# Three stages on one core: loads of the gates, decays as bias, transposes in pieces and the first units in another order

## The chip, the core and the metric

The kernel runs on one core of a Trainium2 chip. The metric is the time of one execution on the device, in microseconds (us). The core has TensorE (PE, its weight loads are PEld), VectorE (DVE), ScalarE (ACT), GpSimd (POOL) and SyncE (SP), which here issues every DMA. Each engine works through its own list of instructions in order and waits for others by semaphores.

## The reference

Three stages in a row, all in fp32. The first is an mLSTM over 4 batches of 8 heads (32 rows), 768 tokens, 40 channels:

```python
for t in range(S):
    m_new = np.maximum(f_gate[:, :, t] + m, i_gate[:, :, t])
    f_stab = np.exp(f_gate[:, :, t] + m - m_new)
    i_stab = np.exp(i_gate[:, :, t] - m_new)
    m = m_new
    C = f_stab * C + i_stab * einsum('bhd,bhe->bhde', v_t, k_t)
    n = f_stab * n + i_stab * k_t
    y[:, :, t] = sigmoid(o_gate_t) * (C q_t) / max(|n . q_t|, 1)
```

The result, as 3072 tokens of 320 channels, goes through a soft mixture of experts (logits with phi, a softmax over the tokens that fills 32 slots, 8 experts of 4 slots with a relu network of width 1024, a softmax over the slots that brings them back) and then through x -> relu(x W_in)^2 W_out with a width of 2048.

## The kernel before

The recurrence is computed in chunks of 128 tokens, 6 of them. In a chunk the state is not stepped: scores k.q of all pairs of tokens are multiplied by a matrix of decays and masked (causal), then multiplied by v; what comes from earlier chunks is added from a state of 40 x 41 per row. The 32 rows are in 11 groups of up to 3; a group and a chunk make a unit, 66 in all. The units of groups 0 and 1 come first, two chunks of one and two of the other in turn (units 0 to 11), then group after group.

Ahead of that stands the preparation `prep` for a pair of chunks (steps are named by a digit for the pair, 1 to 3, and a letter). Gates of all 32 rows lie on partitions three times over (96), tokens along the free axis. "f" (L359) is a scan of forget gates, "i" (L375) the input gates less it, "m" (L365) the running maximum, "h" (L387) its negative cast to bf16, "p" (L370) the maximum before the chunk. "b" and "a" (L375) subtract the chunk's last and previous maximum, "B" and "A" (L378) are the exponentials of that. "r" (L381), "u" (L394), "l" (L375) and "v" (L396) make the parts of the maximum in bf16 that TensorE will broadcast. "q" transposes everything to tokens on partitions (two matmuls L355, copied by ScalarE at L356 into `qt3`): columns 0 to 31 are the biases of the decay exponentials, 32 to 63 the weights of the values, 64 to 95 the decays of the earlier state. D0 to D2 (`prep_dec`, L403 to L423) make the states' decays.

For a unit n: Mn broadcasts the maximum (TensorE, L448, three matmuls), En takes three exponentials with a bias from `qt3` (ScalarE, L462), Kn masks them (GpSimd, L469), Tn are the scores (TensorE, L479), pn their product (VectorE, L491, "P"), Un and Cn the state's update (TensorE L510, VectorE L526 and L541, decays masked on GpSimd L557), W the values times their weights (GpSimd, L435). Products with the values (L582) are done for two units together, those with the state (L567) for each; L603, L612 and L619 add them. L701 is the tanh that makes the sigmoid of the output gates.

The order of all engines in this first part is written by hand: a loop over the units does M of unit i+3, T of i+2, U of i+1, then a slice of the string START, then P of i+2, E of i+3 and the rest. The string's first part, up to the first bar, runs ahead of the loop, each further part in one iteration. "~n" are n warm-ups: matmuls of the identity whose result is never read (L203). From unit 12 on the string plays no part. Later the spare time of the engines is filled with steps of the second and third stage and with weights cast ahead.

Loads go in program order into one queue. Keys are loaded into a block-diagonal form (`kbd`, 120 partitions, three blocks), whose zeros VectorE (L285) and ScalarE (L288) write first.

Of the kernel before, what the change touches and what calls it, by code (L numbers as in the profile page):

```python
# [13 lines left out]
AF = mybir.ActivationFunctionType  # L14
# [3 lines left out]
NEG = -1e30  # L18
# [14 lines left out]
W8 = 1  # L33
WO = (3, 6, 9)
LAST = {3: "PADNgGG", 2: "gGGA", 1: ""}
START = "~36 1f 1i 1m 1h 1p 1b 1aG 1B 1r 1u 1A 1v D0 2f 1l T0 T1 1q M0 2i E0 W0 K0 D0 M1 E1 ~6 2m D0 2p 2b 2aG K1 W2 P0 2h D0 2B 2r 2u U0 P1 M2 2v E2 2A 2l K2 C0 ~7 | 3f 3i D1 ~6 | D1 2q 3m 3h 3p | D1 3b 3aG 3B 3r | 3u D1 3A 3l 3v | D2 3q | D2 | D2 | D2 X |"
REBIAS = 2.0**-112


# [5 lines left out]
def kernel(  # L45
# [240 lines left out]
    for g, cs in ((1, halves[0]), (0, halves[1]), (1, halves[1])):
        z = kbd[g][:, :, cs]
        nc.scalar.activation(z, ident[0 : 3 * D, 0:1].unsqueeze(2).to_broadcast(list(z.shape)), AF.Copy, scale=0.0)  # L288
    for g in range(2):
        load_kb(g, halves[0])  # L290
        load_q(g, halves[0])
        load_kv(g)
    for g in range(2):
        load_kb(g, halves[1])
        load_q(g, halves[1])
    nc.sync.dma_start(out=phs, in_=phi)
    load_x(0, range(NC))
# [4 lines left out]
    )  # L302

    rst = gt(96, [NC, L])
    nc.gpsimd.memset(rst, 1.0)
    nc.gpsimd.memset(rst[:, :, 0:1], 0.0)
    dl = gt(96, [NC, L])
    nc.gpsimd.memset(dl, 0.0)
    nc.gpsimd.memset(dl[:, 0, 0:1], NEG)
    mprev = gt(96, [NC, 1])  # L310
    nc.gpsimd.memset(mprev, NEG)
    nc.gpsimd.memset(hm, 1.0)
    nc.gpsimd.affine_select(
        out=hm, in_=hm, pattern=[[-D, 3]], compare_op=ALU.is_ge, fill=0.0, base=0, channel_multiplier=1
# [6 lines left out]
        nc.gpsimd.memset(rmask[32 * r : 32 * r + 32, r : r + 1], 1.0)  # L321
    nc.gpsimd.memset(selJ, 0.0)
    nc.gpsimd.tensor_copy(selJ[:, :, 0:8], ident[0:32, 0:32].rearrange("p (j i) -> p j i", j=4))
    nc.vector.tensor_reduce(out=gmask, in_=gj, axis=AX.X, op=ALU.add)
    nc.vector.tensor_reduce(out=gs3, in_=gj.rearrange("p g j -> p j g"), axis=AX.X, op=ALU.add)
    nc.vector.tensor_copy(hsel, gs3.unsqueeze(2).to_broadcast([32, 3, D]))
    for r in range(4):
        rs = slice(32 * r, 32 * r + 32)
        nc.vector.tensor_copy(selF[rs, :], ident[rs, rs])
    nc.vector.tensor_copy(sel96, selF[0:96])  # L330

    def flat(t):
        return t.rearrange("p c s -> p (c s)")
# [65 lines left out]

    def prep_dec(c0, c1):  # L400
# [1278 lines left out]
```

## Time and profile before

| | us |
|---|---|
| median of 3 runs | 376.63 (375.51 to 376.94) |
| profiled execution | 376.6 |
| its span (first to last instruction) | 374.9 |
| TensorE busy | 364.6 (97%) |
| VectorE busy | 263.5 (70%) |
| ScalarE busy | 258.5 (69%) |
| GpSimd busy | 102.8 (27%) |
| chain that ended last, TensorE's share | 85% |

Busy times are sums over the whole span; GpSimd works in the first half only. TensorE's share counts the warm-ups as work, and the granted clock is 1.00 throughout. The chain follows the last instruction back, at each step to what released it. The stretch that the change touches is the first 30 us or so; a row of the timeline gives the start, the duration, the line and the operation of one or several instructions of the same form.

### The profile page before, as it was taken

How to read it: one execution, taken by the hardware profiler on the slowest of the kernel's cores; microseconds unless marked ns; L12 is line 12 of the kernel's file. 1: busy time of each engine (PE TensorE's matmuls, PEld its weight loads, DVE VectorE, ACT ScalarE, POOL GpSimd, SP SyncE). 2: the span in 40 equal slices, each digit the busy share in tenths (PEclk: the TensorE clock that was granted, in tenths of full speed). 3: DMA queues.
4: the chain of work that ended last, by engine and by line, in shares of the span. 5: the costliest groups of instructions: out<-in, count | busy, mean ns of one | idle time of the engine just before them, and what ended most of it. 6: DMA issues, size and time to landing. Idle time of an engine off the chain costs nothing.

```text
span 374.9 us, 10814 instructions
## 1 busy us (share of the span) xinstructions
PE 364.6 (97%) x4203; PEld 325.1 (87%) x4203; DVE 263.5 (70%) x597; ACT 258.5 (69%) x594; POOL 102.8 (27%) x205
## 2 busy tenths in 40 slices
PE   8999999998899999999999999999999999999996
PEld 6789888888779885345999999999999999999995
DVE  8879889986998587886799655555555555555551
ACT  7798776678566865766798756676675666667661
POOL 5576986775687573000000000000000000000000
PEclk9999999999999999999999999999999999999999
DMA  5887998999979999893000200020020001002002
GB/s 183 266 315 217 344 328 238 298 332 347 295 199 397 311 353 365 313 380 130 2 0 2 70 3 0 2 71 2 0 72 1 0 11 60 3 0 73 0 2 70
DMA packets 23004, 56.73 MB, mean 151 GB/s; under 512 B 2865, under 2 KB 9865, under 8 KB 22569
## 3 DMA queue, kind: packets, MB, share of 16 engines
q1 hardware_dynamic: 22953, 56.04, 44.3%
q8 instruction: 33, 0.54, 0.6%
q14 instruction: 18, 0.15, 0.1%
HBM read 52.10 MB, written 3.93 MB: 149 GB/s over the span
## 4 chain that ended last, share of the span: by engine, by line
PE 85%; DVE 5%; ACT 4%; POOL 3%; issue 2%; POOLq 0%
PE ps_mb L1574 19%; PE ps_st L1574 17%; PE ps_lt L1574 9%; PE ps_st L479 8%; PE ps_o L1501 4%; PE ps_o L567 4%; PE ps_o L582 4%; PE ps_st L1389 2%; PE ps_m L1501 2%; ACT w L462 2%; POOL w L469 2%; PE ps_mb L448 2%; PE ps_lt L203 2%; PE ps_st L510 2%; PE ps_lt L733 2%
## 5 line engine op out<-in xcount | busy, mean ns | idle before, releaser
L1525 DVE CAST hi<-ring 128x512 fp32r<-128x512 f32 x93 | 39.7, 427 | 62.0 <-ACT ring L1524 51.8
L1526 DVE TENSOR_TENSOR los<-ring,hi 128x512 fp32r<-128x512 f32 x96 | 66.6, 693 | 9.8
L462 ACT ACTIVATE w<-ps_mb,qt 128x128 f32<-128x128 f32 x192 | 56.4, 368 | 11.5 <-PE ps_mb L448 7.0
L1506 ACT ACTIVATE ring<-ps_o 128x512 f32<-128x512 f32 x64 | 38.2, 597 | 35.0 <-PE ps_o L1501 35.0
L1524 ACT ACTIVATE ring<-ring 128x512 f32<-128x512 f32 x93 | 58.8, 632 | 3.0
L479 PE MATMUL ps_st<-par 120*128 120x128 f32 (+1 forms) x384 | 57.0, 284 | 0.7 <-DVE cu L541 0.6
L1574 PE MATMUL ps_mb<-wohlh,hi 128*128 128x320 f32 x160 | 49.4, 310 | 0.0
L1574 PE MATMUL ps_mb<-wohll,hi 128*128 128x320 f32 x160 | 49.3, 309 | 0.0
L1574 PE MATMUL ps_mb<-wohlh,los 128*128 128x320 f32 x160 | 49.2, 309 | 0.0
L479 PEld LDWEIGHTS ps_st<-par 120*128 120x128 f32 (+1 forms) x384 | 47.9, 191 | 1.2 <-PE ps_mb L448 0.9
L491 DVE TENSOR_TENSOR p<-ps_st,w 128x384 f32<-128x384 f32 (+1 forms) x66 | 35.6, 539 | 16.8 <-POOL w L469 8.2
L469 POOL TENSOR_SCALAR_AFFINE_SELECT w<-w 128x384 f32<-128x384 f32 (+1 forms) x66 | 38.3, 581 | 25.1 <-ACT w L462 23.6
L1574 PE MATMUL ps_st<-wohll,hi 128*128 128x320 f32 x144 | 44.6, 310 | 0.0
L1574 PE MATMUL ps_st<-wohlh,hi 128*128 128x320 f32 x144 | 44.5, 309 | 0.0
L1574 PE MATMUL ps_st<-wohlh,los 128*128 128x320 f32 x144 | 44.5, 309 | 0.0
L1506 ACT ACTIVATE ring<-ps_m 128x512 f32<-128x512 f32 x32 | 19.1, 598 | 19.1 <-PE ps_m L1501 19.1
L1574 PEld LDWEIGHTS ps_mb<-wohll,hi 128*128 128x128 f32 x160 | 29.9, 187 | 1.5
L1574 PEld LDWEIGHTS ps_mb<-wohlh,hi 128*128 128x128 f32 x160 | 30.0, 188 | 0.0
L1574 PEld LDWEIGHTS ps_mb<-wohlh,los 128*128 128x128 f32 x160 | 30.0, 188 | 0.0
L1574 PEld LDWEIGHTS ps_st<-wohll,hi 128*128 128x128 f32 x144 | 27.0, 187 | 2.1 <-issue 0.6
L1574 PEld LDWEIGHTS ps_st<-wohlh,los 128*128 128x128 f32 x144 | 27.1, 188 | 0.0
L1574 PEld LDWEIGHTS ps_st<-wohlh,hi 128*128 128x128 f32 x144 | 27.1, 188 | 0.0
(318 smaller groups left out, 762.2 us busy)
## 6 DMA issues: line engine op xcount, KB each, us to landing
ring<-in_w_dram SPq DMA_DIRECT2D x32, 320.0 KB
stage<-in_w_in_dram SPq DMA_DIRECT2D x10, 512.0 KB
par<-in_w_dram SPq DMA_DIRECT2D x6, 640.0 KB
ring<-in_w_dram SPq DMA_DIRECT2D x6, 640.0 KB
out_dram<-ring SPq DMA_DIRECT2D x24, 160.0 KB
par<-in_k_s_dram SPq DMA_DIRECT2D x9, 360.0 KB
x<-in_o_gate_dram SPq DMA_DIRECT2D x9, 320.0 KB
par<-in_k_t_dram SPq DMA_DIRECT2D x23, 120.0 KB
```

Source lines behind the costliest of these rows:

```text
L462: nc.scalar.activation(w[:, j, :], mb[:, 128 * j : 128 * j + 128], AF.Exp, bias=qt3[:, c, h0 + j : h0 + j + 1])
L469: nc.gpsimd.affine_select(out=w, in_=w, pattern=[[0, nh], [1, 128]], compare_op=ALU.is_ge, fill=0.0, base=0, channel_multiplier=-1)
L479: nc.tensor.matmul(st[:, 128 * j : 128 * j + 128], lhsT=kbd[g % 2][0:nd, j, ts_], rhs=qin[g][0:nd, ts_], start=True, stop=True,)
L491: nc.vector.tensor_tensor(out=p, in0=sts.pop((g, c))[:, 0 : nh * 128].rearrange("p (n t) -> p n t", n=nh), in1=ws.pop((g, c)), op=ALU.mult,)
L567: nc.tensor.matmul(pos[g, c // 2][:, o0 : o0 + nv], lhsT=qin[g][0:nd, 128 * c : 128 * c + 128], rhs=cbds[g, c - 1][0:nd], start=True, stop ...
L582: nc.tensor.matmul(po[t0 : t0 + 32, o0 : o0 + DV], lhsT=p[:, j, t0 : t0 + 32], rhs=vin[g][:, c, j, :], start=True, stop=True,)
L1501: nc.tensor.matmul(t, lhsT=gst[n][:, 128 * k : 128 * k + 128], rhs=cst[tg], start=True, stop=True)
L1506: nc.scalar.activation(r, t, AF.Relu)
L1524: nc.scalar.activation(r, r, AF.Square)
L1525: nc.vector.tensor_copy(hi, r)
L1526: eng.tensor_tensor(out=lo, in0=r, in1=hi.bitcast(F32), op=ALU.subtract)
L1574: nc.tensor.matmul(acc[u][:, 0:DM], lhsT=l_[:, 128 * u : 128 * u + 128], rhs=wohl[r_, f // 8][:, f % 8, :], start=(f == 0 and a == 0), sto ...
```

## The change

It has these parts. The gates of the first two chunks are loaded alone and first, those of the other four behind the first keys and queries; keys, queries and values come in parts of two and four chunks. The zeros are written in smaller pieces, a part of them by GpSimd. The differences "a" and "b" go: the exponentials take the maximum as a bias per partition, and for that run chunk by chunk (32 x 128); "n" makes the negative of the last maximum. The transposes "q" become three pieces: "s" (columns 0 to 31, copied by ScalarE), "t" (32 to 63) and "w" (64 to 95), both copied by VectorE. Some copies of the identity move from VectorE to GpSimd, and reductions that prepare the decays move back in the order ("H"). The string START is written anew, with 33 warm-ups in place of 55.

```diff
-START = "~36 1f 1i 1m 1h 1p 1b 1aG 1B 1r 1u 1A 1v D0 2f 1l T0 T1 1q M0 2i E0 W0 K0 D0 M1 E1 ~6 2m D0 2p 2b 2aG K1 W2 P0 2h D0 2B 2r 2u U0 P1 M2 2v E2 2A 2l K2 C0 ~7 | 3f 3i D1 ~6 | D1 2q 3m 3h 3p | D1 3b 3aG 3B 3r | 3u D1 3A 3l 3v | D2 3q | D2 | D2 | D2 X |"
+START = "~13 1f 1i 1s ~9 1m 1h 1p 1n 1r 1u 1v H D0 1l T0 M0 T1 1B 2f M1 E0 H 2i 1t K0 W0 D0 E1 ~9 2m 1A 2h P0 2r D0 2u K1 W2 U0 D0 P1 2l 2v 2p 2n M2 E2 K2 C0 L ~1 | 3f 3i D1 2s 2B 1w ~1 | 2t D1 3m | D1 3h 2A 3r | 3u D1 2w 3l 3v 3p 3n | 3A D2 | 3s 3B 3t D2 | D2 3w | D2 X |"
...
+    load_gates(0, 2)
+    halves = slice(0, 2 * L), slice(2 * L, S)
     nc.vector.memset(kbd[0][:, :, halves[0]], 0.0)
...
+    for g in (1, 0):
+        for j in range(3):
+            zero(g, j, halves[1 - g])
+    zeros = []
+    for j in range(3):
+        zeros.append(lambda j=j: nc.gpsimd.memset(kbd[1][:, j, halves[1]], 0.0))
+    load_kb(0, halves[0])
+    load_q(0, halves[0])
+    load_gates(2, NC)
+    load_kv(0, 0, 2)
+    load_kb(1, halves[0])
+    load_q(1, halves[0])
+    load_kv(1, 0, 2)
+
+    def load_second():
+        for g in range(2):
+            load_kb(g, halves[1])
+            load_q(g, halves[1])
+            load_kv(g, 2, NC)
+        nc.sync.dma_start(out=phs, in_=phi)
+        load_x(0, range(NC))
...
-        nc.vector.tensor_copy(selF[rs, :], ident[rs, rs])
-    nc.vector.tensor_copy(sel96, selF[0:96])
+        if r < 3:
+            nc.vector.tensor_copy(sel96[rs, :], ident[rs, rs])
+        nc.gpsimd.tensor_copy(selF[rs, :], ident[rs, rs])
...
-        def qt():
-            t = ltb
+        def qt(r=0, n=96):
+            t = bank("o") if n == 64 and c0 == 0 else ltb
             for c in range(c0, c1):
-                nc.tensor.transpose(t[:, 96 * (c - c0) : 96 * (c - c0) + 96], q3[:, c, :], ident[0:96, 0:96])
-            nc.scalar.copy(qt3[:, cs, :], t[:, 0 : 96 * w].rearrange("p (c s) -> p c s", s=96))
+                nc.tensor.transpose(t[:, n * (c - c0) : n * (c - c0) + n], q3[0:n, c, :], ident[0:n, 0:n])
+            tv = t[:, 0 : n * w].rearrange("p (c s) -> p c s", s=n)
+            (nc.vector.tensor_copy if r else nc.scalar.copy)(qt3[:, cs, r:n], tv[:, :, r:])
...
         def exp(r):
-            return lambda: nc.scalar.activation(q3[r : r + 32, cs], q3[r : r + 32, cs], AF.Exp)
+            def go():
+                for c in range(c0, c1):
+                    src, b, k = (q3, mlast, 1.0) if r == 32 else (mm, mprev, -1.0)
+                    nc.scalar.activation(
+                        q3[r : r + 32, c], src[r : r + 32, c], AF.Exp, bias=b[r : r + 32, c], scale=k
+                    )
+
+            return go
...
-            "a": sub(q3[64:96, cs], mprev[64:96, cs].to_broadcast([32, w, L]), mm[64:96, cs]),
-            "b": sub(q3[32:64, cs], q3[32:64, cs], last),
+            "n": last,
...
+            "s": qt32,
+            "t": lambda: qt(32, 64),
+            "w": lambda: qt(64),
```

Line numbers of the changed kernel are higher by about 50 in this part: scores are L529, products with the values L632, "s" is L391 and L392, "t" and "w" are L384 and L386, the half exponentials L422, tanh L751.

VectorE's rows at the start of the preparation, before; L329 and L330 copy the identity, L359 is "f", the first L375 "i", L365 "m", the second L375 "b", L381 "r", the last L375 "l":

```order
L329 COPY selF<-ident 32x32 x4
L330 CAST sel_105<-selF 96x32
L359 SCALAR_TENSOR_TENSOR ring<-ring 96x256
L375 TENSOR_TENSOR ring<-ring 96x256
L364 COPY ring<-ring 96x1
L365 SCALAR_TENSOR_TENSOR ring<-ring 96x256
L370 TENSOR_TENSOR ring<-ring 96x1
L375 TENSOR_TENSOR ring<-ring 32x256
L381 SCALAR_TENSOR_TENSOR ring<-ring,M_112 96x256
L403 TENSOR_TENSOR ring<-ring 32x2
L359 SCALAR_TENSOR_TENSOR ring<-ring 96x256
L375 TENSOR_TENSOR M_112<-ring,M_112 32x256
```

The same place in the changed kernel, where L395 is "f", the first L411 "i", L401 "m", L414 "n", L429 "r" and the last L411 "l":

```order
L353 CAST sel_105<-ident 32x32 x3
L395 SCALAR_TENSOR_TENSOR ring<-ring 96x256
L411 TENSOR_TENSOR ring<-ring 96x256
L400 COPY ring<-ring 96x1
L401 SCALAR_TENSOR_TENSOR ring<-ring 96x256
L406 TENSOR_TENSOR ring<-ring 96x1
L414 TENSOR_SCALAR ring<-ring 32x2
L429 SCALAR_TENSOR_TENSOR ring<-ring,M_112 96x256
...
L453 TENSOR_TENSOR ring<-ring 32x2
L411 TENSOR_TENSOR M_112<-ring,M_112 32x256
L395 SCALAR_TENSOR_TENSOR ring<-ring 96x256
```

The copies of `selF` are gone from VectorE, "b" is replaced by the 32x2 row L414, and the scan of the second pair of chunks now follows "l", where it stood ahead of it.

ScalarE's rows from the decay of pair 3 (L404) past E7 to E8, the last row, before:

```order
L404 ACTIVATE ring<-ring 32x2
L356 COPY qt_113<-ps_lt 128x192
L462 ACTIVATE w<-ps_mb,qt_113 128x128 x3
L603 COPY ring<-ps_o 128x123
L701 ACTIVATE x<-x 128x640
L462 ACTIVATE w<-ps_mb,qt_113 128x128 x3
```

The same place of the changed kernel, E7 and E8 being the two rows L512:

```order
L454 ACTIVATE ring<-ring 32x2
L512 ACTIVATE w<-ps_mb,qt_113 128x128 x3
L653 COPY ring<-ps_o 128x123
L751 ACTIVATE x<-x 128x640
L392 COPY qt_113<-ps_m 128x2x32
L422 ACTIVATE ring<-ring 32x128 x2
L512 ACTIVATE w<-ps_mb,qt_113 128x128 x3
```

The copy of transposes ahead of E7 has gone, and behind the tanh (L751) the copy of "s" and both exponentials of "B" stand ahead of E8.

TensorE's rows around T7, before: L355 are the transposes of pair 3, L448 the last of the broadcasts ahead of T7 (L479), then U6 (L510) and the products:

```order
L510 MATMUL ps_st<-wv,par_70 120x123
L355 MATMUL ps_lt<-ident,ring 128x96 x2
L567 MATMUL ps_o<-ring,par_70 128x123
...
L448 MATMUL ps_mb<-M_112,sel_105 128x128
L479 MATMUL ps_st<-par_71 128x128 x3
L510 MATMUL ps_st<-wv,par_71 120x123
L582 MATMUL ps_o<-par_70,p 32x41 x24
L567 MATMUL ps_o<-ring,par_70 128x123
```

And in the changed kernel, T7 being L529 and U6 L560:

```order
L498 MATMUL ps_mb<-M_112,sel_105 128x128
L529 MATMUL ps_st<-par_71 128x128 x3
L560 MATMUL ps_st<-wv,par_71 120x123
L391 MATMUL ps_m<-ident,ring 128x32 x2
L384 MATMUL ps_lt<-ident,ring 128x64 x2
L632 MATMUL ps_o<-par_70,p 32x41 x24
L617 MATMUL ps_o<-ring,par_70 128x123
```

The transposes have moved from ahead of T7 to behind U6, where they are two pairs, "s" (L391) and "t" (L384), ahead of the products with the values of units 4 and 5. The third pair, "w", stands one iteration later.

## Rows read from the trace of the kernel before

**Rows 1.** Windows: busy us (instructions) by engine, granted clock, DMA share, GB/s.
```profile
0.00:10.00 10.00, 8.51 (x58) 6.80 (x59) 8.14 (x23) 7.28 (x13) 5.10 (x26) 1.00 0.62 191
...
30.00:50.00 20.00, 19.19 (x426) 17.81 (x428) 17.30 (x41) 16.06 (x48) 16.14 (x29) 1.00 0.90 278
...
70.00:90.00 20.00, 19.90 (x400) 17.89 (x398) 18.00 (x46) 15.89 (x50) 13.52 (x24) 1.00 0.99 313
```

**Rows 2.** Chain of waits, 0 to 60 us: start us, us, what.
```profile
1.42 6.51 PE ps_lt L203 x36
...
23.24 0.72 PE ps_st L479 x6
```

**Rows 3.** Timeline of SP's DMA issues: start us, us, what.
```profile
1.24 0.41 SPq L283 DMA_DIRECT2D ring<-in_i_gate_dram  x1
...
15.59 1.34 SPq L238 DMA_DIRECT2D x<-in_o_gate_dram  x3
```

**Rows 4.** Timeline of VectorE: start us, us, line, operation, [idle before].
```profile
2.49 1.33 DVE L329 COPY selF<-ident 32x32 f32<-32x32 f32 x4
...
4.97 0.42 DVE L375 TENSOR_TENSOR ring<-ring 96x256 f32<-96x256 f32 x1 [0.25 <-DMA ring<-in_i_gate_dram]
...
5.56 0.69 DVE L365 TENSOR_TENSOR_SCAN ring<-ring 96x256 f32<-96x256 f32 x1
...
6.54 0.42 DVE L375 TENSOR_TENSOR ring<-ring 32x256 f32<-32x256 f32 x1
...
11.53 0.56 DVE L491 TENSOR_TENSOR p<-ps_st,w 128x384 f32<-128x384 f32 x1 [0.44 <-POOL w L469]
12.01 0.17 DVE L423 COPY dec<-ps_m 120x22 f32<-120x22 f32 x1
```

**Rows 5.** Timeline of ScalarE.
```profile
8.12 0.41 ACT L378 ACTIVATE ring<-ring 32x256 f32<-32x256 f32 x1
8.55 0.40 ACT L396 CAST M<-ring 32x256 bf16<-32x256 f32 x1
...
9.83 1.66 ACT L462 ACTIVATE w<-ps_mb,qt 128x128 f32<-128x128 f32 x6
...
22.73 0.29 ACT L356 COPY qt<-ps_lt 128x192 f32<-128x192 f32 x1
22.93 0.85 ACT L462 ACTIVATE w<-ps_mb,qt 128x128 f32<-128x128 f32 x3
23.69 0.23 ACT L603 COPY ring<-ps_o 128x123 f32<-128x123 f32 x1
23.83 0.73 ACT L701 ACTIVATE x<-x 128x640 f32<-128x640 f32 x1
24.47 0.84 ACT L462 ACTIVATE w<-ps_mb,qt 128x128 f32<-128x128 f32 x3
```

**Rows 6.** Timeline of TensorE; the first row is the stretch 2.4 to 3.4 us alone.
```profile
2.04 1.70 PE L203 MATMUL ps_lt<-ident 128*128 128x256 bf16 x7
...
9.28 0.50 PE L448 MATMUL ps_mb<-M,sel 96*128 96x128 bf16 x6
...
22.14 0.33 PE L355 MATMUL ps_lt<-ident,ring 96*128 96x96 f32 x2
...
23.08 0.89 PE L479 MATMUL ps_st<-par 120*128 120x128 f32 x6
...
24.11 0.67 PE L582 MATMUL ps_o<-par,p 128*32 128x41 f32 x48
```

**Rows 7.** Timeline of GpSimd.
```profile
2.61 0.74 POOL L308 MEMSET ring<- 96x768 f32 x1
...
5.01 0.46 POOL L323 COPY selJ<-ident 32x32 f32<-32x32 f32 x1
```

**Rows 8.** Waits: engine, line, releaser, us in total, times, longest.
```profile
POOL wv L435 <- DMA par<-in_v_s_dram: 1.9, 1, 1.9
...
PE ps_o L582 <- issue: 1.4, 1, 1.4
```

More of the change, by code (lines that the diff above doesn't have):

```diff
@@ L281, with load_gates, zero @@
     nc.scalar.activation(dm, dm, AF.Exp)
-    nc.sync.dma_start(out=fg.rearrange("p c s -> p (c s)"), in_=f_gate)
-    nc.sync.dma_start(out=ig.rearrange("p c s -> p (c s)"), in_=i_gate)
-    halves = slice(0, S // 2), slice(S // 2, S)
-    nc.vector.memset(kbd[0][:, :, halves[0]], 0.0)
[L286 to L297, printed above, removed]
+    def load_gates(c0, c1):
+        for t, src in ((fg, f_gate), (ig, i_gate)):
+            nc.sync.dma_start(
+                out=t[:, c0:c1].rearrange("p c s -> p (c s)"), in_=src[:, L * c0 : L * c1]
+            )
+    def zero(g, j, cs):
+        z = kbd[g][:, j, cs]
+        nc.scalar.activation(z, ident[0 : 3 * D, 0:1].to_broadcast(list(z.shape)), AF.Copy, scale=0.0)
+    load_gates(0, 2)
+    halves = slice(0, 2 * L), slice(2 * L, S)
+    nc.vector.memset(kbd[0][:, :, halves[0]], 0.0)
+    for g in (1, 0):
[18 more added lines that the diff above has]
+        load_x(0, range(NC))
     nc.gpsimd.memset(gj, 1.0)
@@ L304 @@
     rst = gt(96, [NC, L])
-    nc.gpsimd.memset(rst, 1.0)
-    nc.gpsimd.memset(rst[:, :, 0:1], 0.0)
     dl = gt(96, [NC, L])
-    nc.gpsimd.memset(dl, 0.0)
-    nc.gpsimd.memset(dl[:, 0, 0:1], NEG)
     mprev = gt(96, [NC, 1])
-    nc.gpsimd.memset(mprev, NEG)
+    mlast = gt(96, [NC, 1])
+    for c0, c1 in ((0, 2), (2, NC)):
+        nc.gpsimd.memset(rst[:, c0:c1], 1.0)
+        nc.gpsimd.memset(rst[:, c0:c1, 0:1], 0.0)
+        nc.gpsimd.memset(dl[:, c0:c1], 0.0)
+        if c0 == 0:
+            nc.gpsimd.memset(dl[:, 0, 0:1], NEG)
+            nc.gpsimd.memset(mprev, NEG)
+        else:
+            for z in zeros:
+                z()
     nc.gpsimd.memset(hm, 1.0)
@@ L323, with heads @@
     nc.gpsimd.tensor_copy(selJ[:, :, 0:8], ident[0:32, 0:32].rearrange("p (j i) -> p j i", j=4))
-    nc.vector.tensor_reduce(out=gmask, in_=gj, axis=AX.X, op=ALU.add)
-    nc.vector.tensor_reduce(out=gs3, in_=gj.rearrange("p g j -> p j g"), axis=AX.X, op=ALU.add)
-    nc.vector.tensor_copy(hsel, gs3.unsqueeze(2).to_broadcast([32, 3, D]))
     for r in range(4):
         rs = slice(32 * r, 32 * r + 32)
-        nc.vector.tensor_copy(selF[rs, :], ident[rs, rs])
-    nc.vector.tensor_copy(sel96, selF[0:96])
+        if r < 3:
+            nc.vector.tensor_copy(sel96[rs, :], ident[rs, rs])
+        nc.gpsimd.tensor_copy(selF[rs, :], ident[rs, rs])
+    def heads():
+        nc.vector.tensor_reduce(out=gmask, in_=gj, axis=AX.X, op=ALU.add)
+        nc.vector.tensor_reduce(out=gs3, in_=gj.rearrange("p g j -> p j g"), axis=AX.X, op=ALU.add)
+        yield
+        nc.vector.tensor_copy(hsel, gs3.unsqueeze(2).to_broadcast([32, 3, D]))
     def flat(t):
@@ L348, in prep, with qt32 @@
         tail = mm[:, c0 - 1, L - 1 : L] if c0 else 0.0
-        last = mm[32:64, cs, L - 1 : L].to_broadcast([32, w, L])
         tt = {"D": nc.vector.tensor_tensor, "G": nc.gpsimd.tensor_tensor}
-        def qt():
-            t = ltb
+        def qt(r=0, n=96):
+            t = bank("o") if n == 64 and c0 == 0 else ltb
             for c in range(c0, c1):
-                nc.tensor.transpose(t[:, 96 * (c - c0) : 96 * (c - c0) + 96], q3[:, c, :], ident[0:96, 0:96])
-            nc.scalar.copy(qt3[:, cs, :], t[:, 0 : 96 * w].rearrange("p (c s) -> p c s", s=96))
+                nc.tensor.transpose(t[:, n * (c - c0) : n * (c - c0) + n], q3[0:n, c, :], ident[0:n, 0:n])
+            tv = t[:, 0 : n * w].rearrange("p (c s) -> p c s", s=n)
+            (nc.vector.tensor_copy if r else nc.scalar.copy)(qt3[:, cs, r:n], tv[:, :, r:])
+        def qt32():
+            t = bank("m")
+            for c in range(c0, c1):
+                nc.tensor.transpose(t[:, 32 * (c - c0) : 32 * (c - c0) + 32], q3[0:32, c, :], ident[0:32, 0:32])
+            nc.scalar.copy(qt3[:, cs, 0:32], t[:, 0 : 32 * w].rearrange("p (c s) -> p c s", s=32))
         def f_scan():
@@ L375, in sub, with last @@
             return lambda e="D": tt[e](out=o_, in0=a, in1=b, op=ALU.subtract)
+        def last():
+            nc.vector.tensor_scalar(
+                out=mlast[32:64, cs], in0=mm[32:64, cs, L - 1 : L], scalar1=-1.0, scalar2=None, op0=ALU.mult
+            )
         def exp(r):
-            return lambda: nc.scalar.activation(q3[r : r + 32, cs], q3[r : r + 32, cs], AF.Exp)
+            def go():
+                for c in range(c0, c1):
+                    src, b, k = (q3, mlast, 1.0) if r == 32 else (mm, mprev, -1.0)
+                    nc.scalar.activation(
+                        q3[r : r + 32, c], src[r : r + 32, c], AF.Exp, bias=b[r : r + 32, c], scale=k
+                    )
+            return go
         def rest():
@@ L922 @@
     begin["W"] = lambda n: e_wv(units[int(n)][0], 0, 2)
+    hd = heads()
+    begin["H"] = lambda: next(hd, None)
+    begin["L"] = load_second
     begin["X"] = lambda: nc.vector.tensor_copy(sel4, selF.unsqueeze(1).to_broadcast([128, 4, 32]))
```

## The prediction

> **What bounds the kernel now.** I read the windows first [rows 1]. From 30 us on TensorE works 19.19 of 20 us: it alone sets the pace, with 0.8 us of slack, and in 70 to 90 us the DMA share is 0.99 beside it. In 0 to 10 us TensorE's 8.51 us are mostly warm-ups, so a busy TensorE means nothing there; the chain of waits [rows 2] begins with the 36 warm-ups, runs through all four engines in turn (scans on VectorE, exponentials on ScalarE, masks on GpSimd, scores on TensorE) and lies on TensorE for most of its length from the scores at 23.24 us on. From unit 12 on the instructions stand in the same order before and behind the change, so the change is worth what it does to the moment at which TensorE becomes busy without a break, less what a later wait swallows. I follow one signal: how much earlier or later the same step starts (its lead). The profiled run took 376.6 us (span 374.9 and 1.7 around it), the same as the median of 376.63, so the sum is made against 376.6.
>
> **Gates.** The DMA of the input gates is issued at 1.24 us [rows 3], second in its queue in both kernels. The first subtraction starts at 4.97 us, after a wait of 0.25 for it [rows 4]. Now 384 of the 576 KB of gates no longer come with or ahead of it. If the 3.3 us from its issue's end to its use are latency alone, nothing is won; if bytes alone, 384 KB at the 191 GB/s of the first window [rows 1] are 2.0 us. I take the middle, 1.0, so that the subtraction starts at about 4.0 us. VectorE is then free: ahead of it stand a memset of two thirds the size, three 32x32 casts in place of four copies of 1.33 us together and a cast, and a scan of the form of the row at 5.56, 0.69 us [rows 4].
>
> **Loads.** Keys, queries and values in chunks of 2 and 4 in place of 3 and 3 or 6 make six more DMAs, about 0.4 us of issue each by [rows 3]: 2.4 us. They stand behind what the first units read, but ahead of the load of the output gates, issued at 15.59 us before [rows 3] and first used at 23.83 [rows 5]: 8 us of cover, of which 5.8 stay. Cost nothing; without that cover the tanh would be late one for one. The zeroing in smaller pieces (the same area) lies on ScalarE and GpSimd while the gates are under way.
>
> **Differences as bias.** The subtraction "b" (0.42 at 6.54 [rows 4]) stood between the scan and the rest term; in its place stands a 32x2 tensor_scalar, 0.1 to 0.42: above is what it replaces, below the nearest small row (0.17 at 12.01), which I take. On ScalarE the exponential of "A" (0.41 at 8.12) no longer stands ahead of the cast "v" at 8.55 [rows 5], nor on VectorE the next scan (0.69) ahead of "l". All of this lies on the way to the broadcasts M0, at 9.28 [rows 6]: 9.28 - 1.0 - 0.42 + 0.17 - 0.41 = 7.6 us, a lead of 1.7. Behind "v" ScalarE has a 32x2 exponential (0.2) and two half-size ones ahead of E0. A 32x128 exponential with a bias isn't in the trace: between 0.28 (a sixth of E0's 1.66, [rows 5]) and 0.41 (the whole 32x256); I take 0.30, near the row of its width. E0 then starts at about 8.1 for 9.83: lead 1.7. The first mask also waits for GpSimd's setup, which ended at 5.47 [rows 7] and now has three memsets of 120x512, 0.49 each by scaling the 0.74 of 96x768, and four 32x32 copies, 0.1 to 0.46 each (its own row at 5.01): end at 7.3 to 8.8. The first three of E0's six exponentials end at 8.95, so it is covered, barely at the upper end. Ahead of the first product p0 VectorE has the second pair's scan, as before: p0 at about 10.1 for 11.53 [rows 4], lead 1.4.
>
> GpSimd's 32x32 copies now lie beside VectorE's scans and subtractions. In the rows the one at 5.01 took 0.46 beside a subtraction that kept its 0.42 [rows 4, 7], so VectorE loses nothing. The Trainium skill, page "SBUF — State Buffer", section "SBUF: two separate sides", says that a VectorE operation with two SBUF inputs and a GpSimd operation that reads SBUF share a pair of ports as an exclusive lock, and that the later one blocks. By it four copies might each stand once ahead of a VectorE row, an estimate of up to 1.8 us, and the lead would be gone; by the row the loss is nil.
>
> **Transposes in three pieces.** For each pair of chunks one TensorE pair (0.33 at 22.14) and one ScalarE copy (0.29 at 22.73) become three pairs, one ScalarE copy and two VectorE copies [rows 5, 6]. VectorE gets two copies of 0.17 to 0.29 and the tensor_scalar, and loses 0.42: 0.1 to 0.33 a pair. ScalarE has four half exponentials (1.2) for two (0.82): 0.4. TensorE has two more pairs at up to 0.33. For the two pairs of chunks ahead of unit 7 I take 0.7 of lead lost, between VectorE's alone (0.2) and TensorE's alone (1.3), since the engines take turns on the chain. So E7 starts at 22.2 for 22.93 and T7 at 22.4 for 23.08 [rows 5, 6].
>
> **The slice "3s 3B 3t".** Here a new wait is made. TensorE's order is now T7, U6, transposes "s", transposes "t", then the products L632 of units 4 and 5 and the rest. "t" reads what the exponentials "B" write, and on ScalarE these stand behind E7, a copy (L603 before, 0.23), a tanh of 128x640 (0.73) and the copy of "s". Before, all transposes of this pair were done ahead of T7, and from E7's start to E8's were 1.54 us [rows 5]. Now, from 22.2: 1.54, 0.2 for the copy of "s", 0.6 for two half exponentials; the data of "t" are there at 24.55. TensorE is through with "s" at about 23.6 (T7's 0.89, U6 and a pair from 22.4) and stands 1.0 us. With 0.3 for the pair "t" the products start at 24.85 for 24.11 [rows 6], 0.75 late. The third pair, "w", comes on top in the next iteration, 0.1 to 0.33. So TensorE is about 0.85 late where it becomes the only bound.
>
> **What is given back.** There is slack of 0.8 in 30 to 50 us, and at 92.8 us GpSimd waits 1.9 us for values with the DMAs full [rows 1, 8]. A delay of TensorE that doesn't delay transfers is swallowed there; but transfers start when buffers come free, so part of it does. I take half: + 0.4, so 376.6 + 0.4 = **377.0 us**. Bounds: the gates' lead 0 or 2.0, half swallowed, 0.5 either way; half exponentials at 0.28 or 0.41, 0.2; the lateness swallowed wholly or not at all, 0.4: 375.9 to 378.1 for the forecast alone.
>
> **Warm-ups** fall from 55 to 33. 22 at 0.11 us are 2.4 us of TensorE for which nothing waited, as the chain names no warm-up behind the first 36. Their work counts nothing; the clock is rival 2.
>
> **Rivals.**
> 1. The lead survives. If the third pair's "B" finds ScalarE free (the tanh in another place, or E7 earlier than worked out), the stall of 1.0 is gone: 0.85 late becomes 0.15 early, with the gates' upper bound 1.15 early, 375.4 us. If the 13 warm-ups ahead of units 3 and 4 (7 and 6, now 1 and 1) did hold the broadcasts behind them, another 1.4: 374.0. For it: TensorE is close to a bound here, and a term of 1.0 rests on the order of a few ScalarE rows. Against: "t" needs "B" by its data, and the tanh's 0.73 stands ahead of it. Chance 0.27, of which 0.17 below 374.75.
> 2. The slower one: TensorE's clock. The first warm-ups start 213 ns apart (seven in 1.70 us [rows 6]), which is the level of 1.2 GHz; 36 take 6.51 [rows 2], so the later ones went at 2.4. Now TensorE stands between 13 warm-ups and its next work, and where 7 and 6 filled gaps there is one each. If the clock falls there, the scores (0.89) and broadcasts (half of 0.50) of four units [rows 6] take 4.6 us more; half of that on the chain, 2.3: 379.3. It decides if the level is the lower one behind unit 3. Against: an idle of 1.4 us at L582 [rows 8] stands in a stretch with a granted clock of 1.00. The Trainium skill, "TensorE: Matmul & The Clock Gate", section "Part 1: The HAM clock gate (the "warmup" mystery)", says that the lower level is the default and that idleness brings it back; by it this rival would hold if the gaps are long enough, and no run here shows such a fall yet. Chance 0.13.
> 3. The end doesn't move: 376.6. Bytes and order of transfers behind 30 us are the same, and at a share of 0.99 they may set the pace whatever TensorE does at 25 us. Against: the wait of 1.9 us is the only one of its kind, and TensorE is busy above nine tenths around it. Chance 0.17.
>
> **How the numbers follow.** The forecast has 0.43, the rivals 0.27, 0.13 and 0.17. A measurement of this kernel tells about 0.5% from no change: below 374.75 or above 378.5. Faster: 0.17, from the first rival. Slower: the second's 0.13 and 0.04 from beyond the forecast's upper edge. Same: the rest, 0.66. With a tenth left out on either side the range is 374.8 to 379.2.
>
> **What would show it.** In the changed profile: the first subtraction at 4.0 us, M0 at 7.6, E0 at 8.1, p0 at 10.1; near 23.6 us a wait of TensorE for ScalarE of about 1.0 at the transposes L384; the products L632 of units 4 and 5 at 24.85; no matmul at the 1.2 GHz level behind 9 us. I am wrong if that wait is under 0.3 us, if these products start before 24.11, or if slow matmuls stand between 9 and 20 us.

## The result: slower by about 1.2%

| | us |
|---|---|
| changed kernel, 6 runs | median 380.0 (378.82 to 383.67) |
| kernel before, 6 runs | median 376.0 (374.9 to 376.94) |
| ratio | 1.0117, 95% interval 1.0086 to 1.0147 |
| profiled run of the changed kernel | 383.67, span 382.0, mean granted clock 0.985 |

The forecast of 377.0 and its range, up to 379.2, missed it. The windows of the changed kernel (columns as in [rows 1]) show where the profiled run differs at a glance:

```profile
0.00:10.00 10.00, 8.25 (x55) 6.06 (x55) 7.90 (x22) 8.26 (x23) 8.13 (x36) 1.00 0.60 175
10.00:20.00 10.00, 8.08 (x98) 7.06 (x97) 7.11 (x22) 7.40 (x26) 4.95 (x9) 0.78 0.99 308
20.00:30.00 10.00, 9.25 (x143) 8.35 (x143) 5.04 (x18) 5.90 (x20) 3.43 (x9) 0.71 0.48 181
30.00:50.00 20.00, 19.19 (x385) 17.78 (x385) 16.74 (x43) 17.03 (x49) 14.34 (x28) 1.00 0.80 258
...
70.00:90.00 20.00, 19.36 (x393) 16.63 (x394) 17.91 (x45) 13.55 (x45) 14.88 (x27) 1.00 0.94 300
```

TensorE's granted clock is 0.78 and 0.71 between 10 and 30 us: here it ran part of the time at the lower level, 1.2 GHz. But that is not the whole loss. Other runs of the same kernel had a granted clock of 1.00 and still took 379.3 and 380.25 us. So I read two traces of it: this one, and a second one of a run at 1.00 all along (span 378.9, 380.62 us).

The beginning answers to [rows 4 to 6]. VectorE's first subtraction, TensorE's first broadcasts, ScalarE's first exponentials of unit 0 and the first product, in the first trace:

```profile
1.65 1.53 DVE L353 CAST sel<-ident 32x32 bf16<-32x32 f32 x3
3.21 0.69 DVE L395 TENSOR_TENSOR_SCAN ring<-ring 96x256 f32<-96x256 f32 x1
3.93 0.42 DVE L411 TENSOR_TENSOR ring<-ring 96x256 f32<-96x256 f32 x1
...
10.03 0.53 DVE L541 TENSOR_TENSOR p<-ps_st,w 128x384 f32<-128x384 f32 x1
```

```profile
7.12 0.34 PE L498 MATMUL ps_mb<-M,sel 96*128 96x128 bf16 x3 [0.30 <-DVE M L411]
```

```profile
8.01 1.66 ACT L512 ACTIVATE w<-ps_mb,qt 128x128 f32<-128x128 f32 x6
```

The subtraction starts 1.04 us earlier than before, the broadcasts 2.16, the exponentials 1.82, the product 1.50. The lead is there, and nearly to the size forecast. To see where it goes, I followed one row, the product of scores and weights (L491 before, L541 now), through all units. Starts in us, from VectorE's timelines; "second" is the changed kernel's second trace, the others are experiments told below:

| unit | before | changed | second | fewwarm | warm | nobar | slice | mend |
|---|---|---|---|---|---|---|---|---|
| 0 | 11.53 | 10.03 | 10.61 | 12.91 | 10.67 | 10.04 | 10.02 | 10.03 |
| 2 | 15.84 | 14.23 | 14.82 | 16.87 | 14.87 | 14.26 | 14.22 | 14.45 |
| 3 | 17.93 | 17.54 | 18.15 | 18.96 | 18.19 | 17.12 | 17.54 | 17.19 |
| 5 | 21.53 | 24.16 | 22.22 | 22.81 | 22.26 | 21.05 | 22.66 | 21.12 |
| 6 | 23.32 | 26.52 | 23.44 | 24.35 | 23.48 | 22.27 | 23.88 | 22.34 |
| 7 | 24.47 | 29.54 | 26.73 | 26.23 | 26.77 | 25.56 | 26.34 | 24.44 |
| 8 | 26.40 | 32.19 | 29.38 | 27.97 | 29.42 | 28.21 | 28.56 | 27.01 |
| 12 | 33.36 | 38.60 | 35.78 | 34.94 | 35.82 | 34.62 | 34.97 | 33.42 |
| 39 | 87.10 | 93.00 | 90.26 | 88.69 | 89.61 | 88.39 | 89.83 | 87.74 |
| 42 | 94.16 | 99.69 | 96.24 | 94.08 | 96.36 | 93.98 | 96.79 | 94.35 |
| 63 | 137.69 | 144.65 | 140.81 | 137.61 | 139.65 | 137.66 | 140.31 | 137.99 |

In the second trace a lead of 1.02 us at unit 2 is a lag of 0.22 at unit 3, and a lag of 0.12 at unit 6 is 2.26 at unit 7. Those are two places. The first is on TensorE, in the first iteration of the loop (second trace):

```profile
12.29 0.30 PE L391 MATMUL ps_m<-ident,ring 32*128 32x32 f32 x2
12.52 0.39 PE L384 MATMUL ps_lt<-ident,ring 96*128 96x96 f32 x2
14.94 0.27 PE L203 MATMUL ps_lt<-ident 128*128 128x256 bf16 x1 [2.04 <-DVE qt L386]
15.05 0.33 PE L498 MATMUL ps_mb<-M,sel 96*128 96x128 bf16 x3
15.22 0.89 PE L529 MATMUL ps_st<-par 120*128 120x128 f32 x6
```

The engine stands 2.04 us before one warm-up of 0.27. The bracket names what released it: VectorE's copy L386. The slice is "3f 3i D1 2s 2B 1w ~1". "1w" transposes into the bank `ps_lt`; "~1" writes the same bank, and so has to wait until VectorE has copied it out. VectorE has other work in front of that copy, the scan and subtraction of "3f 3i":

```profile
13.42 0.68 DVE L395 TENSOR_TENSOR_SCAN ring<-ring 96x256 f32<-96x256 f32 x1
14.13 0.56 DVE L411 TENSOR_TENSOR ring<-ring 96x256 f32<-96x256 f32 x1
14.61 0.14 DVE L453 TENSOR_TENSOR ring<-ring 32x2 f32<-32x2 f32 x1
14.69 0.20 DVE L386 COPY qt<-ps_lt 128x64 f32<-128x64 f32 x1
14.82 0.54 DVE L541 TENSOR_TENSOR p<-ps_st,w 128x384 f32<-128x384 f32 x1
...
16.63 0.23 DVE L386 COPY qt<-ps_lt 128x64 f32<-128x64 f32 x1 [1.02 <-PE ps_lt L384]
```

A matmul whose result nobody reads is thus a barrier between two engines, and broadcasts, scores and all the rest of TensorE's list stand behind it. The last row shows how it reaches the product of unit 3 (18.15): the transposes "2t" are late on TensorE too, and VectorE, which has their copy ahead of that product in its list, stands 1.02 us for them.

The second place is the slice "3s 3B 3t" that the prediction named. ScalarE and TensorE in the second trace:

```profile
23.66 0.84 ACT L512 ACTIVATE w<-ps_mb,qt 128x128 f32<-128x128 f32 x3
24.41 0.24 ACT L653 COPY ring<-ps_o 128x123 f32<-128x123 f32 x1
24.55 0.74 ACT L751 ACTIVATE x<-x 128x640 f32<-128x640 f32 x1
25.20 0.21 ACT L392 COPY qt<-ps_m 128x64 f32<-128x64 f32 x1
25.44 0.69 ACT L422 ACTIVATE ring<-ring 32x128 f32<-32x128 f32 x2
```

```profile
23.83 0.89 PE L529 MATMUL ps_st<-par 120*128 120x128 f32 x6
24.55 0.38 PE L560 MATMUL ps_st<-wv,par 128*120 128x123 f32 x2
24.86 0.31 PE L391 MATMUL ps_m<-ident,ring 32*128 32x32 f32 x2
25.89 0.56 PE L384 MATMUL ps_lt<-ident,ring 64*128 64x64 f32 x2 [0.73 <-ACT ring L422]
26.39 0.67 PE L632 MATMUL ps_o<-par,p 128*32 128x41 f32 x48
```

TensorE waits 0.73 us for the half exponentials, as foreseen, and the products L632 start at 26.39 for 24.11 [rows 6]: 2.28 late, where 0.74 had been forecast. E7 itself, at 23.66, is 0.73 later than in [rows 5], not 0.7 earlier. The product of unit 7 pays on another engine:

```profile
26.50 0.23 DVE L386 COPY qt<-ps_lt 128x64 f32<-128x64 f32 x1 [1.52 <-PE ps_lt L384]
...
26.73 0.54 DVE L541 TENSOR_TENSOR p<-ps_st,w 128x384 f32<-128x384 f32 x1
```

Its scores are done at 24.72 and its masked weights at 25.16 (GpSimd L519), but the copy of "t" stands ahead of it in VectorE's list, and VectorE waits 1.52 us for those transposes.

### The profile page after: what moved, and what is told of

Its sections match the earlier page's. It is cut to its first block, busy times and chain, and to the rows that moved or that the text cites. A ratio compares the mean times of both kernels' runs of the same rounds, so it can differ in the third digit from the quotient of the medians.

```text
span 382.0 us, 10829 instructions
## 1 busy us (share of the span) xinstructions
PE 368.0 (96%) x4193; PEld 327.4 (86%) x4193; DVE 262.5 (69%) x601; ACT 259.7 (68%) x603; POOL 102.8 (27%) x212
## 3 DMA queue, kind: packets, MB, share of 16 engines
HBM read 52.10 MB, written 3.93 MB: 147 GB/s over the span
## 4 chain that ended last, share of the span: by engine, by line
PE 77%; DVE 10%; POOL 4%; DMA 3%; issue 3%; ACT 2%; SPq 0%; POOLq 0%; DVEq 0%; ACTq 0%
PE ps_mb L1627 18%; PE ps_st L1627 17%; PE ps_lt L1627 9%; PE ps_st L529 6%; PE ps_o L1554 4%; DVE p L541 3%; PE ps_o L632 3%; PE ps_o L617 2%; PE ps_st L1442 2%; PE ps_m L1554 2%; DMA par<-in_v_s_dram 2%; DVE x L714 2%; PE ps_st L560 2%; PE ps_mb L498 2%; POOL w L519 1%
## 5 line engine op out<-in xcount | busy, mean ns | idle before, releaser
L512 ACT ACTIVATE w<-ps_mb,qt 128x128 f32<-128x128 f32 x192 | 56.5, 371 | 12.5 <-PE ps_mb L498 7.3
L529 PE MATMUL ps_st<-par 120*128 120x128 f32 (+1 forms) x384 | 59.0, 290 | 1.4 <-DMA par<-in_v_s_dram 1.1
L529 PEld LDWEIGHTS ps_st<-par 120*128 120x128 f32 (+1 forms) x384 | 49.8, 197 | 1.9 <-issue 1.3
L541 DVE TENSOR_TENSOR p<-ps_st,w 128x384 f32<-128x384 f32 (+1 forms) x66 | 35.5, 537 | 18.2 <-PE ps_st L560 7.9
L519 POOL TENSOR_SCALAR_AFFINE_SELECT w<-w 128x384 f32<-128x384 f32 (+1 forms) x66 | 37.0, 560 | 29.5 <-ACT w L512 26.5
```

Source lines behind the costliest of these rows:

```text
L512: nc.scalar.activation(w[:, j, :], mb[:, 128 * j : 128 * j + 128], AF.Exp, bias=qt3[:, c, h0 + j : h0 + j + 1])
L519: nc.gpsimd.affine_select(out=w, in_=w, pattern=[[0, nh], [1, 128]], compare_op=ALU.is_ge, fill=0.0, base=0, channel_multiplier=-1)
L529: nc.tensor.matmul(st[:, 128 * j : 128 * j + 128], lhsT=kbd[g % 2][0:nd, j, ts_], rhs=qin[g][0:nd, ts_], start=True, stop=True,)
L541: nc.vector.tensor_tensor(out=p, in0=sts.pop((g, c))[:, 0 : nh * 128].rearrange("p (n t) -> p n t", n=nh), in1=ws.pop((g, c)), op=ALU.mult,)
```

## The experiments

The theories at the start: clock (the loss is the fall of TensorE's clock) against order (the loss is where the pieces of the transposes and the warm-ups stand). Ratios are against the kernel before, run on the same chip at the same time, with the 95% interval.

**The changed kernel again.** No edit.

> The changed kernel once more, to see how its time spreads and to get a second trace. Theory clock: the loss comes from a fall of TensorE's clock near 16 us; a run whose granted clock is 1.00 all along then takes 376 to 377 us, one with a fall 380 to 384. Theory order: the loss comes from where the pieces of the transposes stand (TensorE waits near 13 us and near 28 us), so a run at a clock of 1.00 still takes 378.5 to 380, and the fall adds to it.

Measured: 380.4 us (4 runs, 380.22 to 380.62), ratio 1.0097 (1.0062 to 1.0133). The profiled run at a clock of 1.00 took 380.62. Theory clock falls as the main cause; the time lies at or just above the range of theory order. The fall does cost something, though: at unit 8 the trace with the fall is 2.81 us behind the one without (32.19 and 29.38), although it was 0.58 ahead at unit 0. The scores just behind the fall, in the first trace:

```profile
17.10 0.79 PE L617 MATMUL ps_o<-ring,par 120*128 120x123 f32 x2
17.68 0.53 PE L498 MATMUL ps_mb<-M,sel 96*128 96x128 bf16 x3
18.00 1.59 PE L529 MATMUL ps_st<-par 120*128 120x128 f32 x6
```

and the same ones in the second:

```profile
17.12 0.48 PE L617 MATMUL ps_o<-ring,par 120*128 120x123 f32 x2
17.44 0.33 PE L498 MATMUL ps_mb<-M,sel 96*128 96x128 bf16 x3
17.61 0.89 PE L529 MATMUL ps_st<-par 120*128 120x128 f32 x6
```

**Gaps filled with warm-ups (warm).**

```diff
-... C0 L ~1 | 3f 3i D1 2s 2B 1w ~1 | ...
+... C0 L ~7 | 3f 3i D1 ~6 2s 2B 1w ~1 | ...
```

> The changed kernel with 7 warm-ups in place of 1 at the end of the part ahead of the loop, and 6 in place of 1 in the first iteration, there ahead of the transposes, so that they fill the gap near 13 to 14 us. Theory clock: no fall in any run, and 376 to 377.5 us. Theory order: the fall may go, but the time stays at that of the changed kernel's runs without it, 378.5 to 380 us.

Measured: 378.17 us, 1.0056 (1.0032 to 1.0081); 11 of 12 runs had a granted clock of 0.998 or more. The time lies between the ranges of the two theories, nearer to that of theory order. In the table its units 7 and 8 stand as in the second trace (26.77, 29.42): the one warm-up behind "1w" was left in, and TensorE still stands before it:

```profile
12.73 0.82 PE L203 MATMUL ps_lt<-ident 128*128 128x256 bf16 x6
13.48 0.30 PE L391 MATMUL ps_m<-ident,ring 32*128 32x32 f32 x2
13.71 0.38 PE L384 MATMUL ps_lt<-ident,ring 96*128 96x96 f32 x2
14.99 0.27 PE L203 MATMUL ps_lt<-ident 128*128 128x256 bf16 x1 [0.90 <-DVE qt L386]
```

The gap got shorter, its end did not move. That row is what turned theory order into two separate mends. Why the time fell all the same is not shown: at unit 30 this trace and the second are level (72.39 and 72.34).

**"3s 3B" one iteration earlier (slice).**

```diff
-... | 3A D2 | 3s 3B 3t D2 | D2 3w | ...
+... | 3A 3s 3B D2 | 3t D2 | D2 3w | ...
```

> The changed kernel with the transposes 's' and the exponentials 'B' of the third pair one iteration earlier, so that 't' finds its data ready. Theory order: TensorE's wait for the half exponentials (0.7 us in the changed kernel's trace) goes and the time falls by about 0.7 to 1.0 us against the changed kernel. Theory clock: no difference over 0.3 us, since the loss was made before unit 5.

Measured: 378.63 us, 1.0052 (1.0027 to 1.0077). The wait for the half exponentials is gone; theory order is borne out there, though the time fell by more than its 0.7 to 1.0 us. Between units 6 and 7 pass 2.46 us, for 3.29 in the second trace. Here too the gap before the warm-up (1.38 us) stood in the trace, and a fall of the clock behind it (0.66 between 15 and 20 us).

**The kernel before with fewer warm-ups (fewwarm).** 13, 6, 1 and 1 for 36, 6, 7 and 6.

> The kernel before with 13, 6, 1 and 1 warm-ups in place of 36, 6, 7 and 6, nothing else. Theory clock: the clock falls near 10 to 20 us as in the changed kernel, and the time is 379 to 383 us. Theory order: TensorE's clock rises later, but the time stays within 0.5% of 376.0 us, since the transposes still stand as they did.

Measured: 377.35 us, 1.0026 (1.0003 to 1.0049): theory order. Fewer first warm-ups do cost something, otherwise than I thought, since the scores behind them run at the lower level:

```profile
1.42 2.95 PE L203 MATMUL ps_lt<-ident 128*128 128x256 bf16 x13 [1.42 <-POOL dm L280]
7.75 2.90 PE L479 MATMUL ps_st<-par 120*128 120x128 f32 x12 [3.37 <-DVE ring L381]
```

The twelve scores take 2.90 us here, for 1.50 in the kernel before, and the first product is 1.38 late. The granted clock of 5 to 10 us reads 1.00 even so; the lower level shows in the durations alone. And one thing more: at unit 39 this kernel is 1.59 us behind the kernel before, at unit 42 it is 0.08 ahead. The wait for values at 92.8 us [rows 8] is where it caught up: the kernel before waits 1.9 us there, this one 0.3, and both go on at the same time (92.84 and 92.77). This is the trace of a run of 376.95 us; what the median has beyond that it can't show.

**The warm-up ahead of the transposes (nobar).** One token moved.

```diff
-... | 3f 3i D1 2s 2B 1w ~1 | ...
+... | 3f 3i D1 2s 2B ~1 1w | ...
```

> The changed kernel with the one warm-up of the first iteration ahead of the transposes 'w' instead of behind them. Behind them it writes the bank that VectorE has yet to copy out, so TensorE stands 1.4 to 2.0 us until VectorE gets there, and the broadcasts of unit 3 stand behind it. Theory barrier: the wait goes, products 3 to 7 come 0.4 to 1.0 us earlier and the time falls by as much, to 379.4 to 380. Theory ScalarE: the broadcasts weren't late for the exponentials, which wait for VectorE anyway, and nothing changes (380.4).

Measured: 377.92 us, 1.0028 (1.0008 to 1.0049), 10 of 12 runs at a clock of 0.999 or more. The barrier is gone:

```profile
12.58 0.28 PE L203 MATMUL ps_lt<-ident 128*128 128x256 bf16 x1
12.70 0.33 PE L384 MATMUL ps_lt<-ident,ring 96*128 96x96 f32 x2
13.14 0.33 PE L498 MATMUL ps_mb<-M,sel 96*128 96x128 bf16 x3
```

Units 5 to 8 come 1.17 us earlier than in the second trace, but 0.57 of it is there at unit 0 already: this run began like the first trace of the changed kernel, with 10.04, and the second with 10.61 (its nine warm-ups took 2.10 us, for 1.40 in the first trace and 1.47 here, so the clock rose later). The barrier itself is the rest, 0.6 us, counted from unit 0 on. That is what theory barrier expected of the products. The medians differ by more, 2.5 us, and the time is below the 379.4 to 380 that was expected. It is not the clock: among runs at 0.998 or more the medians are 380.42 and 377.82. A smaller lag is made up later (below), in a trace that is of the fastest of the 12 runs, though (376.69).

**Both mends (mend).** warm without the warm-up behind "1w", and slice.

```diff
-... C0 L ~1 | 3f 3i D1 2s 2B 1w ~1 | ... | 3A D2 | 3s 3B 3t D2 | ...
+... C0 L ~7 | 3f 3i D1 ~6 2s 2B 1w | ... | 3A 3s 3B D2 | 3t D2 | ...
```

> The changed kernel with both mends together: warm-ups filled in (7 and 6, none behind the transposes 'w'), and 's' and 'B' of the third pair one iteration earlier. If the barrier and the wait for the half exponentials are separate losses, they add: 376.8 to 377.8 us. If VectorE's longer list is the loss, it stays at 378 or above, as each of the two mends alone.

Measured: 376.08 us for 376.95 of the kernel before, 0.998 (0.9964 to 0.9997); the granted clock is 0.998 or more in all 12 runs. The two losses are separate and add: from the 1.0097 of the changed kernel nobar takes 0.0069 and slice 0.0045, and this kernel, which also fills the gaps, stands 0.0117 below it. From nobar to mend unit 7 moves from 25.56 to 24.44. Both traces begin alike (10.04 and 10.03). TensorE stands no more ahead of "t", and E8 (24.44) and L632 (24.02) are as early as in the kernel before [rows 5, 6]:

```profile
23.45 0.38 PE L560 MATMUL ps_st<-wv,par 128*120 128x123 f32 x2
23.76 0.34 PE L384 MATMUL ps_lt<-ident,ring 64*128 64x64 f32 x2
24.02 0.67 PE L632 MATMUL ps_o<-par,p 128*32 128x41 f32 x48
```

The time is below the range that was expected if the losses add, 376.8 to 377.8. This is the one version that is faster than both kernels, by about 0.2% of the kernel before, close to what can be told, and its trace (377.01) doesn't explain it: from unit 8 on it is nowhere ahead of the kernel before. The lead of the front is gone here too, 1.50 us at unit 0, 0.03 at unit 7 and none at unit 12; in no version is any of it left there.

**Both mends without filling (nofill).** slice, and the warm-up ahead of "1w" as in nobar; against slice only that one token moved.

> As the last kernel with both mends, but with 1 and 1 warm-ups as in the changed kernel (the second ahead of the transposes 'w'): barrier gone and slice mended, gaps not filled. Theory barrier: the filling is worth nothing once TensorE no longer stands behind the bank; granted clock 1.00 in nearly all runs and 0.998 of the time before, as with both mends. Theory clock: the gap of about 1 us that is left is enough for a fall, clocks of 0.98 to 0.995 in half of the runs and 1 to 3 us more.

Measured: 376.15 us for 376.44, 1.0006 (0.998 to 1.0032); 10 of 12 runs at 0.999 or more. Theory barrier: the fill is worth little once the barrier is gone. The same token is worth 1.0097 to 1.0028 alone and 1.0052 to 1.0006 on top of slice.

**The second and third pair's transposes whole (qwhole).** "2q" and "3q" in the slices of the kernel before.

> The changed kernel with the transposes of the second and third pair of chunks whole again (one pair of matmuls, one copy on ScalarE), in the slices where the kernel before has them; the first pair stays in pieces, the biases stay. Theory pieces: the loss is VectorE's copies and TensorE's waits for them; the product of unit 7 starts 1.5 to 2.5 us earlier than in the changed kernel and the time is 376.5 to 378. Theory bias: the half exponentials on ScalarE are the loss, and the time stays above 379.

Measured: 377.0 us, 1.0002 (0.9983 to 1.002). Theory pieces: the time is that of the kernel before with the biases left in, so the half exponentials are no loss that can be measured. The product of unit 7 comes at 25.39, 1.34 earlier than in the second trace and so a little less than expected. The barrier behind "1w" is still in it: its trace shows a gap of 1.77 us and slow matmuls after it (clock 0.66 between 15 and 20 us). The lag, 1.22 at unit 39, is 0.06 at unit 42, so the barrier's wait is made up where the rest of the lag is gone. What its gap still costs seems to come by way of the clock: 9 of the 12 runs had 0.994 or 0.995 and a median of 377.23, the other three 376.02.

**Third pair whole (whole3), and second and third whole with gaps filled (whole23)**, both without the barrier.

> Both mends, and the third pair's transposes whole again (one pair of matmuls, one copy on ScalarE, in the slice where 't' stood). Theory pieces cost: two pairs of matmuls and two VectorE copies less, so the product of unit 8 starts 0.5 to 1.0 us earlier than with both mends (27.0 us) and the time falls by 0.3 to 0.8 if the lead is carried. Theory swallowed: the wait for the load of values near 92 us takes it, and the time is that of both mends (0.998 of before).

> As the kernel with the second and third pair's transposes whole, with the gaps filled (7 and 6 warm-ups, none behind the transposes 'w' of the first pair). Theory barrier and clock: the product of unit 3 starts near 17.1 us, the fall of the clock in 15 to 20 us goes, and the lead of 1.5 us at the first product is carried past unit 7: 0.994 to 0.998 of before. Theory swallowed: 0.998 to 1.000.

Measured: 377.11 us, 1.001 (0.9989 to 1.0031), and 377.72 us, 1.0026 (1.0004 to 1.0048). In both traces unit 8 is earlier than with both mends (26.75 and 26.64 for 27.01), and the time isn't; both lie above what either theory gave, 0.998 at most and 1.000 at most. Whole3's trace can't tell whether anything was carried: it is of a run of 378.6 us, in which TensorE stands 2.1 us near 88 us at a row for which the profile names no releaser, so that a lag of 0.41 at unit 36 is 2.40 at unit 39. That whole23 is slower than qwhole is not explained.

**The parts ahead of the preparation alone (ahead).** Loads, zeros and copies of the change; order, differences and transposes of the kernel before; 27 first warm-ups.

> The kernel before with the parts of the change that lie ahead of the preparation alone: gates and halves loaded apart, zeros in smaller pieces, copies of the identity moved, and 27 first warm-ups for 36, which would otherwise hold the first broadcasts; differences, transposes and the order of the units as before. The first product should start 0.5 to 1.0 us early. Theory carried: the lead is carried to the end, 375.3 to 375.9 us. Theory swallowed: the waits for DMAs behind 70 us take it, 376.3 us as before.

Measured: 378.64 us, 1.0035 (1.0012 to 1.0059). Neither theory: there is no lead. The first subtraction comes at 3.93, but the first product at 12.85. This run, too, had a fall of the clock, behind a wait of 2.12 us on TensorE (0.50 between 12.5 and 15 us). On GpSimd "a", which the change removes, now stands behind the longer setup:

```profile
7.48 1.27 POOL L354 COPY selF<-ident 32x32 f32<-32x32 f32 x4
8.83 0.61 POOL L411 TENSOR_TENSOR ring<-ring 32x256 f32<-32x256 f32 x1
```

and ScalarE waits for it, with "v" behind:

```profile
9.48 0.41 ACT L419 ACTIVATE ring<-ring 32x256 f32<-32x256 f32 x1 [2.63 <-POOL ring L411]
9.92 0.40 ACT L437 CAST M<-ring 32x256 bf16<-32x256 f32 x1
```

So the edits of the beginning hang together: work may move to GpSimd only because "a" leaves it.

## Why the prediction was wrong

**The front was right.** Subtraction 4.0 (measured 3.93), broadcasts 7.6 (7.12), exponentials 8.1 (8.01), first product 10.1 (10.03 and 10.61). The first of these was luck in part: the forecast took the gates' DMA as what the subtraction waits for, but now it follows straight on the scan, without such a wait, and what holds VectorE are the three casts (1.53 us). GpSimd's four copies took 0.47 each and VectorE's rows beside them kept their 0.42 and 0.69, so VectorE lost nothing there, as the row had said. The Trainium skill, "SBUF — State Buffer", section "SBUF: two separate sides", has the later of two such operations block, and the prediction had made up to 1.8 us of it by estimate; nothing of the kind shows on VectorE.

**The step that failed is "0.7 of lead lost" ahead of unit 7.** It counted each piece by its duration, a few tenths spread over the engines, and took these to alternate. What it left out is what a piece makes others wait for. In fact T7 started 0.75 late and not 0.7 early in the second trace, a miss of 1.4. Of that 0.5 is the start of this run (a lead of 0.92 at unit 0, not 1.4; the first trace has 1.50). 0.6 is one wait, the warm-up behind "1w" (nobar). The rest, 0.3 to 0.4, was not taken apart; in nobar TensorE still waits 0.71 us for VectorE (L669) ahead of T7, so it may be VectorE's longer list. With that token moved, the lag at unit 12 is 1.26, not far from the 0.85 forecast; in the second trace it is 2.42. I counted warm-ups as work and as clock, never as writers of a bank that somebody still reads. The string showed it: "1w ~1" in one slice, and 1w's copy on VectorE, behind a scan.

**The slice "3s 3B 3t" was right in place, and near in size on TensorE.** The wait is 0.73 us for 1.0. That VectorE would stand 1.52 us for the same transposes, ahead of the product of unit 7, was not foreseen. Both mends together bring unit 7 forward by 1.12 against nobar.

**"Half of it is given back" was wrong, and it is the larger part of the miss:** of the 3.6 us between + 0.4 and the measured + 4.0 (medians, and the second trace) about 1.6 are there at unit 12, and 2.0 come behind it. The slack of 0.8 in 30 to 50 us gave nothing back (lag 2.46 at unit 20, 2.48 at unit 33). At the wait of 1.9 us for a DMA near 92.8 us small lags vanish, as rival 3 had it: 1.59 (fewwarm), 1.30 (nobar) and 1.22 (qwhole) at unit 39 are at most 0.06 at unit 42, and the 2.10 of ahead are 0.16. Larger ones aren't shortened by 1.9: 2.51 (warm) becomes 2.20, 2.73 (slice) 2.63 and the second trace's 3.16 becomes 2.08. There the values themselves land later, at 94.8 to 95.5 us, and GpSimd still waits 0.8 to 1.8 us for them. So a lag is swallowed there, or it takes the transfer along; what decides it between 2.1 and 2.5 was not tested. The second trace's 2.08 at unit 42 are 3.12 at unit 63 and 4.0 at the end of the span. 1.1 of that is a wait of TensorE at 128.5 us (L617) that names no releaser, and the 0.9 behind unit 63 stand in the traces of nofill and whole23 as well. What these last 1.9 us have to do with the change stays open.

**Rival 2 came true in part.** It had 0.13 and a price of 2.3; a long fall cost 2.8 where it happened (at unit 8), and the two runs of the changed kernel at a mean clock of 0.985 and 0.986 took 383 us. Short ones, 0.994 or 0.995 in the mean, show no price in the changed kernel (380.58 and 380.22 beside 380.62 and 380.22 at 1.00), but runs with them are 1.2 to 1.6 us slower in qwhole and in the kernel before, which has them in 18 of 93 runs. The gaps of 1.39 (changed), 1.38 (slice) and 1.77 us (qwhole) were followed by slow matmuls, with a granted clock of 0.55, 0.66 and 0.66 between 15 and 20 us; the gap of 2.04 us in the second trace was not (1.00). The Trainium skill, "TensorE: Matmul & The Clock Gate", "Part 1: The HAM clock gate (the "warmup" mystery)", has it that idleness brings the lower level back. These traces agree in three of four cases. With the gap mended, nearly all runs kept the clock (12 of 12 in mend, 10 of 12 in nofill). I judged it by one idle stretch of the kernel before, which stands amid dense work. Of the signs of being wrong, slow matmuls between 9 and 20 us stood in the first trace and not in the second.

**"Warm-ups for which nothing waited" was wrong as well.** The chain in [rows 2] did begin with the 36; and what comes behind 13 of them is slow (fewwarm).

## What to carry over

A matmul for warming has an output, and its bank has readers: put it ahead of transposes into that bank, or give it another one, and check for every filler what it must wait for. When a step is cut into pieces on other engines, write down for each piece what stands ahead of it in that engine's list; a cost per piece says nothing of that. A lag can vanish at a later wait that sets the pace anyway (here up to 2.1 us did), but a larger one can move the awaited transfer too, and then most of it stays. Whether a lead would be lost there these runs don't tell: none was left by then.

## What the runs showed of the hardware that was not expected

Three casts of 32x32 on VectorE took 1.53 us while GpSimd wrote memsets of 0.30 to 0.52 us beside them (first fence of the result), 0.51 each, where a cast of 96x32 lasted 0.18 in the kernel before. And the granted clock fell after a gap of 1.4 us in one run and not after one of 2.0 us in another run of the same kernel.
